# Two pools of the first stretch change places, and the first stretch and batch 1 get a new order

## The chip, the cores and the metric

The kernel runs on one core of a Trainium2 chip. The engines named below are TensorE (PE; its weight loads are listed apart as PEld), VectorE (DVE), ScalarE (ACT), GpSimd (POOL) and SyncE (SP), which here only issues DMAs. The metric is the device time of one execution in microseconds; lower is better. Three executions of the kernel before took 746.87, 747.23 and 748.2 us.

## The reference, cut to what matters

Eight batches of an attention block with a small state, and then a gated feed-forward layer over all 4352 rows that it gives (per batch 512 tokens and 32 state rows, 512 wide):

```python
# x: (B=8, H=8, S=512, D=64), state: (8, 8, 32, 64)
a = softmax(scale * x @ state.T);  xread = a @ state          # tokens read the state
a2 = softmax(scale * state @ x.T); sread = a2 @ x             # the state reads the tokens
rows = concat([xread, sread], axis=2)  -> (B * 544, 512)
xn = rows / rms(rows) * rms_g
g, val = xn @ w_gate, xn @ w_val                              # 512 -> 1536, twice
out = (g * sigmoid(g) * val) @ w_out                          # 1536 -> 512
```

All is float32. The products with w_gate, w_val and w_out are nearly all of the work.

## The kernel before, in words

**Stages.** The kernel works through batch 0 in a first stretch (to about 134 us of the profile), through batches 1 to 7 in seven stretches of about 81 us, and through the state rows of all batches at the end. Since the tokens' reads are `a @ state`, each batch first multiplies the weights with its state (`own_weights`, L753 on PE, copied to a tile `v` by ACT at L765), and then the small matrix `v` with the softmax weights `aT_s`.

**The first stretch** also brings the weights in. They lie in 18 pieces of 1 MB (six pairs of blocks, each gate, val, out). SP loads a piece into one of three `raw` buffers (L241); ACT makes its exponents in two steps (L274 into `lin`, L277 into `ex`), DVE the mantissas (L298) and joins both into the working weight `w_m` or `wo` (L302). A raw buffer is loaded again once its piece is joined, so the load of piece k+3 stands behind the joining of piece k. Each `w_m` is stored back (L305) and fetched again by later batches (L222). For batch 0, `hidden` (L806 on PE, twice a block: gate, then value) fills PSUM banks `pv`, ACT applies silu (L812), DVE multiplies (L816) into `hb`. The projection of batch 0 (L1039 on PE) runs in three groups of blocks; it multiplies blocks of `hb` with blocks of `wo`, and sums of four of them (`group`: POOL at L1023 for the weights, DVE at L1033 for the tokens), and DVE adds the banks up (L1077 to L1088). The last group needs the last two blocks of `hb`.

**What is made for later.** When all weights are joined, DVE makes three sums of `wo` blocks (`weight_sums`, L1114, nine instructions into the tile `wt`), and from `wo` and `wt` the quarter sums for the projections of the later batches (`weight_quarters`, L1226, into three `w2` buffers, which SP stores at L1228 and fetches again at L1217). Batch 1's own token sums (`aT_t`, L828 to L831) are POOL's.

**Batches 1 to 7.** `hidden_seven` runs seven products for each of six pairs of blocks (L910 on PE; ACT copies L957 to L962 and silu L964; DVE additions L973 and L986), `project_twice` the projection as seven outer times seven inner products (L1272 on PE; DVE's quarter sums of tokens L1320 to L1326, half sums L1331; fetches L1217). Beside that DVE, ACT and PE make the next batch's softmax: `x` is turned by DVE (L357), goes out to memory and back in four parts (L359, L364 on ACT's queue, tile `xG`), and PE reads it at L374.

**What sets the order.** Nothing is reordered by a scheduler. Each piece of work is a generator (a stream) named by a letter, and a table of letters says which stream takes its next step: `ORDER` for the first stretch, `FIRST` for batch 1, `PERIOD` for batches 2 to 6. Each engine executes its instructions in that order, and so does SP's queue.

**The places in memory.** Five pools of the first stretch lie one behind the other in the order in which they are opened (L120 to L125): `raws` (three buffers of 8200 bytes per partition), `v_0` (two of 4096: the `v` tiles of batch 0, which L806 reads to its end), `conv` (two of 4096: `ex`), `line` (one of 4096: `lin`), `x_0`. At the first step of a stream `k` (weight sums) or `w` they are closed, and the pools of the later batches are opened on the same place (L1097). The first of these, `late`, holds `wt` (18432 bytes), `hs` (6144) and `aT_t` (3072), 27648 bytes together. Its first instruction waits for the last users of every pool under it.

Of the kernel before, what the change touches and what calls it, by code (L numbers as in the profile page):

```python
# [24 lines left out]
ZERO = 16 * 896  # L25

ORDER = (
    "zzzzaazaaaggggaaaaziizzbzeeeaaaddbbebbaddaabebbsssebzaaaAAAAaAAssabbdAAssdbabbaa"
    "AaAsbbssvbabbebavebbvAddeAehbdhtdeeAAuAdddhAAethuvvveephtddsssWhuesehhssreddstpA"
    "xdvveeWWWuTTrTppxTrrpvpeerrhxppddWAAAAeeddthhAeAAeddStddvvdvhhhuWWxiueppAeeAAddA"  # L30
    "tuhheAddrtuTAeeArxTATTApApeSddSSvxrAvAAvrAppihxShAedppWtheeeuhetdxdvvvddupkkWWWk"
    "kkkkSSShrrSSthhtAAQQQQkpQQxAWuhuTTTSSTAAwrrcppwwwwwxwQQrrSkcpSprrxcQppxwQwcQQ"
)

PERIOD = (
# [4 lines left out]
)  # L40

FIRST = (
    "hhaattavqvhxtaxhahhaauuuqtuqhhtqqtvhqhthhquuqquahuthtqqfuaxhhutxxqqxhthhuaahuhhu"
    "ttthhhqhtxxuukqhkaquuGuvtxhhtaaaukxtaaaGhhtkhhxxhhhGuuuuuttutaaauhhuhuhtuhuutupp"
    "hppppppaaaucuffupkakukkkkppcpppkkpkpppckkaakaalaakkkkkpfkpppcpassaaksaagsppcpkpk"
    "akkkppggappppppppaoogggpsssgcppkakkpssppkooaaassppkskppakkkkoopaafpwwxxxclfwxsxx"
    "coos"
)
LAST = (
    "vhhtnfthhnthxuhguxhtvvhutuhxfhtuthuhhuhhxtuthfxhtuxtxuhxhuhuvtauhhhthxuuthkxthuh"  # L50
# [11 lines left out]
def kernel(  # L62
# [56 lines left out]
    seven["s2"] = ctx.enter_context(tc.tile_pool(name="quarters_h", bufs=2))  # L119
    early = ExitStack()  # L120
    raws = early.enter_context(tc.tile_pool(name="raws", bufs=RAW_AHEAD))
    v_0 = early.enter_context(tc.tile_pool(name="v_0", bufs=2))
    conv = early.enter_context(tc.tile_pool(name="conv", bufs=2))
    line = early.enter_context(tc.tile_pool(name="line", bufs=1))
    x_0 = early.enter_context(tc.tile_pool(name="x_0", bufs=1))  # L125


# [1399 lines left out]
```

## Time and profile before

| | |
|---|---|
| three executions | 746.87, 747.23, 748.2 us; median 747.23 |
| the profiled execution | 747.86 us, of which the span of the core is 746.1 us |
| busy in the span | PE 728.5, DVE 574.4, ACT 350.6, POOL 283.8 us |
| mean granted TensorE clock | 0.993 of full speed |

The span is the time from the first to the last instruction. The profiled execution lies 0.63 us over the median. PE is busy for 98% of the span, so time can be saved only where PE stands still or runs at a lower clock. A row of the timeline has the start and the length in us, engine, line, operation, output and inputs, and in brackets the idle time of that engine just before and what ended it.

### The profile page before, as it was taken

How to read it: one execution, taken by the hardware profiler on the slowest of the kernel's cores; microseconds unless marked ns; L12 is line 12 of the kernel's file. 1: busy time of each engine (PE TensorE's matmuls, PEld its weight loads, DVE VectorE, ACT ScalarE, POOL GpSimd, SP SyncE). 2: the span in 40 equal slices, each digit the busy share in tenths (PEclk: the TensorE clock that was granted, in tenths of full speed). 3: DMA queues.
4: the chain of work that ended last, by engine and by line, in shares of the span. 5: the costliest groups of instructions: out<-in, count | busy, mean ns of one | idle time of the engine just before them, and what ended most of it. 6: DMA issues, size and time to landing. Idle time of an engine off the chain costs nothing.

```text
span 746.1 us, 14468 instructions
## 1 busy us (share of the span) xinstructions
PE 728.5 (98%) x5676; PEld 606.8 (81%) x5676; DVE 574.4 (77%) x972; ACT 350.6 (47%) x610; POOL 283.8 (38%) x376
## 2 busy tenths in 40 slices
PE   8999986999999999999999999999999999999998
PEld 7555554789987898889877997799878987899996
DVE  5878838899946996699848995699569964798862
ACT  5988831256355533654265335552556236511220
POOL 3224023531294126532474228502851267324500
PEclk9999997999999999999999999999999999999999
DMA  7999724785496078706782389318850783063311
GB/s 227 344 317 350 292 114 157 265 308 200 163 283 190 5 304 276 255 11 230 252 309 57 122 312 331 86 36 327 299 185 2 296 265 114 0 223 118 135 51 28
DMA packets 58940, 146.17 MB, mean 196 GB/s; under 512 B 10228, under 2 KB 30200, under 8 KB 51960
## 3 DMA queue, kind: packets, MB, share of 16 engines
q1 hardware_dynamic: 47824, 126.30, 47.5%
q10 hardware_dynamic: 11048, 18.95, 8.5%
q8 instruction: 45, 0.74, 0.4%
q14 instruction: 23, 0.19, 0.1%
HBM read 116.46 MB, written 28.77 MB: 195 GB/s over the span
## 4 chain that ended last, share of the span: by engine, by line
PE 91%; DVE 3%; DMA 3%; ACT 1%; SPq 0%; issue 0%; POOL 0%; DVEq 0%; ACTq 0%
PE f L910 39%; PE f L1272 31%; PE f L1039 5%; PE pv L806 4%; PE pv L753 4%; PE f L1134 2%; PE at L753 2%; DMA raw<-in_moe_w_val_dram 1%; DMA x_b<-in_x_dram 1%; PE at L456 1%; PE at L374 1%; PE f L680 1%; DVE wt L1114 1%; DMA out_dram<-c 1%; DVE w_m L302 1%
## 5 line engine op out<-in xcount | busy, mean ns | idle before, releaser
L910 PE MATMUL f<-aT_s,v 128*128 128x256 f32 x504 | 120.1, 382 | 0.0
L910 PEld LDWEIGHTS f<-aT_s,v 128*128 128x128 f32 x504 | 94.6, 190 | 23.0 <-DVE c L973 5.9
L1300 POOL TENSOR_TENSOR kept<-kept 128x256 f32<-128x256 f32 x28 | 21.2, 756 | 210.7 <-DVE kept L1312 147.1
L973 DVE TENSOR_TENSOR g<-g,f 128x512 f32<-128x512 f32 x84 | 56.7, 685 | 57.6 <-PE f L910 48.6
L910 PE MATMUL f<-aT_t,vs 128*128 128x256 f32 x336 | 86.6, 381 | 0.0
L1272 PE MATMUL f<-w,h 128*128 128x128 f32 x588 | 74.5, 276 | 0.0
L1272 PEld LDWEIGHTS f<-w,h 128*128 128x128 f32 x588 | 69.7, 192 | 4.1 <-DVE eB L662 4.1
L910 PEld LDWEIGHTS f<-aT_t,vs 128*128 128x128 f32 x336 | 63.1, 190 | 10.9 <-issue 1.0
L964 ACT ACTIVATE hb<-g 128x1024 f32<-128x1024 f32 x42 | 44.4, 1058 | 57.3 <-DVE g L973 57.2
L780 POOL TENSOR_TENSOR vs<-v 128x256 f32<-128x256 f32 x42 | 31.3, 746 | 88.5 <-ACT v L765 88.3
L1285 ACT COPY kept<-f 128x512 f32<-128x512 f32 (+1 forms) x56 | 29.3, 532 | 71.3 <-PE f L1272 61.9
L765 ACT COPY v<-pv 128x512 f32<-128x512 f32 x56 | 31.1, 594 | 39.9 <-PE pv L753 39.6
L986 DVE TENSOR_TENSOR hb<-hb,f 128x512 f32<-128x512 f32 (+1 forms) x48 | 31.1, 649 | 18.2 <-PE f L910 18.2
L973 DVE TENSOR_TENSOR c<-c,f 128x512 f32<-128x512 f32 (+1 forms) x48 | 31.3, 653 | 16.4 <-PE f L910 16.2
L910 PE MATMUL f<-aT_s,vs 128*128 128x256 f32 x168 | 43.3, 380 | 0.3 <-ACT c L960 0.3
L910 PE MATMUL f<-aT_t,v 128*128 128x256 f32 x168 | 43.2, 380 | 0.0
L1272 PE MATMUL f<-wo,h 128*128 128x128 f32 x336 | 42.1, 275 | 0.0
L1272 PE MATMUL f<-wo,hb 128*128 128x128 f32 x336 | 42.1, 275 | 0.0
L1272 PEld LDWEIGHTS f<-wo,hb 128*128 128x128 f32 x336 | 40.3, 192 | 0.4
L806 PE MATMUL pv<-aT_s,v 128*128 128x512 f32 x88 | 40.3, 597 | 0.0
L1272 PEld LDWEIGHTS f<-wo,h 128*128 128x128 f32 x336 | 39.8, 192 | 0.0
L986 DVE TENSOR_TENSOR hb<-hb,c 128x512 f32<-128x512 f32 (+1 forms) x48 | 32.9, 685 | 5.7 <-ACT hb L964 4.9
(261 smaller groups left out, 1632.5 us busy)
## 6 DMA issues: line engine op xcount, KB each, us to landing
w_m<-w_d SPq DMA_DIRECT2D x48, 1024.0 KB
w<-t_d SPq DMA_DIRECT2D x49, 576.0 KB
out_dram<-kept SPq DMA_DIRECT2D x30, 256.0 KB
raw<-in_moe_w_val_dram SPq DMA_DIRECT2D x6, 1024.0 KB
raw<-in_moe_w_out_dram SPq DMA_DIRECT2D x6, 1024.0 KB
w_d<-w_m SPq DMA_DIRECT2D x6, 1024.0 KB
x_b<-in_x_dram SPq DMA_DIRECT2D x6, 1024.0 KB
x_d<-xB ACTq DMA_DIRECT2D x6, 1024.0 KB
```

The source lines that it names most:

```text
L753: TE.matmul(out=pv[e][Ns * j:Ns * j + Ns, :], lhsT=stT_g[b][D * e:D * e + D, j, :], rhs=w[D * e:D * e + D, j].rearrange("p m k f -> p (m k ...
L765: SE.copy(v[:, e].rearrange("p m k f -> p (m k f)"), pv[e])
L780: GE.tensor_tensor(out=vs[:, 0], in0=a21, in1=a22, op=ALU.add)
L806: TE.matmul(out=to[0], lhsT=lhs(i, k), rhs=r, start=(i == 0), stop=(i == len(rhs) - 1))
L910: TE.matmul(out=ps[:, i, 0:half], lhsT=l[:, i, :], rhs=r, start=(start and i == 0 and k == 0), stop=(k == len(lhs) - 1), skip_group_check= ...
L964: SE.activation(out=hb[:, 2 * mp:2 * mp + 2, 0:n].rearrange("p m (c t) -> p m c t", c=2), in_=q["g"][:, :, :, 0:half], func=ACTF.Silu if s ...
L973: VE.tensor_tensor(out=to, in0=to, in1=q[ps][:, :, 0:half], op=ALU.add)
L986: VE.tensor_tensor(out=part, in0=part, in1=val, op=ALU.mult)
L1039: TE.matmul(out=bank[:, r, :], lhsT=lhs[:, k, P * r:P * r + P], rhs=rhs[:, k], start=(start and r == 0 and k == 0), stop=(stop and k == 1) ...
L1272: TE.matmul(out=to[half][:, slot, :], lhsT=lhs[:, k, :], rhs=rhs[:, k, :], start=(fresh and n in (0, 4) and k == 0), stop=(k == QM - 1), s ...
L1285: SE.copy(of_half(k, i), banks[name][i])
L1300: GE.tensor_tensor(out=k[:, 4:8:3], in0=k[:, 5:6].to_broadcast([P, 2, QD]), in1=k[:, 4:8:3], op=ALU.add)
```

## The change

Two things. First, the pool `line` is opened ahead of `v_0` and `conv` instead of behind them. The 27648 bytes of `late` then lie over the three `raw` buffers and the first 3 KB of `line`, where they lay over the three `raw` buffers and the first 3 KB of `v_0`. No tile changes its size. Second, the tables `ORDER` and `FIRST` are dealt anew: nearly all streams take the same steps (batch 0 to 1 and the weights' conversion), in another sequence. No instruction is added or removed but for the splitting of runs; `PERIOD`, `LAST` and `STATES` stay.

```diff
 ORDER = (
-    "zzzzaazaaaggggaaaaziizzbzeeeaaaddbbebbaddaabebbsssebzaaaAAAAaAAssabbdAAssdbabbaa"
...
+    "zzzzaazaagaeeaaaazgzzbzaaaebbdeadgbdbbaaedbsssbbzaaaaAAAAAessgdbAbassAAAbbdaaAbb"
...
@@ -119,9 +119,9 @@
     raws = early.enter_context(tc.tile_pool(name="raws", bufs=RAW_AHEAD))
+    line = early.enter_context(tc.tile_pool(name="line", bufs=1))
     v_0 = early.enter_context(tc.tile_pool(name="v_0", bufs=2))
     conv = early.enter_context(tc.tile_pool(name="conv", bufs=2))
-    line = early.enter_context(tc.tile_pool(name="line", bufs=1))
     x_0 = early.enter_context(tc.tile_pool(name="x_0", bufs=1))
```

What the tables do is shown by the order of the instructions on three engines. The names in brackets are the semaphores that an instruction waits for, by the engine that raises them (DMAHW: a DMA).

**DVE, where the weights' last piece is joined (L302 into wo) and the weight sums begin (L1114).** Before:

```order
L302 TENSOR_TENSOR wo<-raw,ex 128x1024 [waits DVE_49,Activation_49]
L816 TENSOR_TENSOR hb<-t,pv 128x512 [waits PE_49,Activation_49]
L1114 TENSOR_TENSOR wt<-wo 128x512 [waits PE_49,DVE_49,Activation_49,Pool_49]
L1114 TENSOR_TENSOR wt<-wo,wt 128x512 [waits DVE_49]
L1114 TENSOR_TENSOR wt<-wo,wt 128x512
L1114 TENSOR_TENSOR wt<-wo 128x512 [waits Pool_49]
```

After:

```order
L302 TENSOR_TENSOR wo<-raw,ex 128x1024 [waits Activation_49]
L1114 TENSOR_TENSOR wt<-wo 128x512 [waits DVE_49]
L1114 TENSOR_TENSOR wt<-wo,wt 128x512 [waits DVE_49]
L1077 TENSOR_TENSOR c_560<-c_560,f 128x512 [waits PE_49]
L816 TENSOR_TENSOR hb<-t,pv 128x512 [waits PE_49,Activation_49]
L1114 TENSOR_TENSOR wt<-wo,wt 128x512
```

The first weight sum no longer waits for PE. Eight of the nine weight sums stood ahead of the last two blocks of hb (L816) before, and seven do now; the L816 of an earlier block is moved in between them.

**PE, the end of batch 0's hidden blocks (L806) and the last group of the projection.** Before:

```order
L806 MATMUL pv<-aT_s,v 128x512 x4
L401 MATMUL at<-part,groups 128x16
L1039 MATMUL f<-wo,hb 128x256 x2
L806 MATMUL pv<-aT_s,v 128x512 x2
L680 MATMUL at<-x_b,e_748 32x64 x32
L325 MATMUL at<-ident,ri 128x128 x4
L1039 MATMUL f<-wo,hb 128x256 x4
L1039 MATMUL f<-group 128x256 x4
```

After:

```order
L806 MATMUL pv<-aT_s,v 128x512 x4
L401 MATMUL at<-part,groups 128x16
L806 MATMUL pv<-aT_s,v 128x512 x2
L1039 MATMUL f<-wo,hb 128x256 x4
L806 MATMUL pv<-aT_s,v 128x512 x2
L1039 MATMUL f<-group,hb 128x256 x4
L1039 MATMUL f<-wo,hb 128x256 x4
L325 MATMUL at<-ident,ri 128x128 x4
```

Behind the last L806 stand now four matmuls on finished sums (L1039 f<-group,hb); before, the L1039 that needs the last two hb blocks came after 36 short ones (L680, L325).

**ACT, batch 1: the last parts of x's way back (L364) and the silu of a pair of blocks (L964).** Before:

```order
L364 DMA xG<-x_d_149 32x4x512
L960 COPY c_1339<-f 128x512
L765 COPY v<-at 128x512 x2
L962 COPY g<-f 128x2x256
L364 DMA xG<-x_d_149 32x4x512 x2
L964 ACTIVATE hb<-g 128x1024
```

After:

```order
L364 DMA xG<-x_d_149 32x4x512 x2
L765 COPY v<-pv 128x512
L962 COPY g<-f 128x2x256
L364 DMA xG<-x_d_149 32x4x512
L964 ACTIVATE hb<-g 128x1024
L364 DMA xG<-x_d_149 32x4x512
```

The last part is issued behind the silu of the third pair of blocks instead of ahead of it. On SP's queue, the load of batch 2's `x` moves ahead of the first store of quarter sums, and in batch 1 the fetch of the fourth set of quarter sums (L1217) stands first, takes one of the three buffers early, and leaves the third fetch to wait until PE is through with the first set; three fetches of 1 MB (L222, for batch 2) stand behind that third fetch now, and stood behind it, without its waiting for PE, before.

More of the change, by code (lines that the diff above doesn't have):

```diff
@@ L27 @@
 ORDER = (
-    "zzzzaazaaaggggaaaaziizzbzeeeaaaddbbebbaddaabebbsssebzaaaAAAAaAAssabbdAAssdbabbaa"
[L29 to L32, printed above, removed]
+    "zzzzaazaagaeeaaaazgzzbzaaaebbdeadgbdbbaaedbsssbbzaaaaAAAAAessgdbAbassAAAbbdaaAbb"
+    "sssbaaevvebbabbbaddbbAvhhAhheeteddeduAAAAdvtpdevveeuhtssepxsAeeddWdhWsuhtAWssAWd"
+    "hrsedvvvurTTppTexTrrrSeppAehAdAddAAxdAAdAeeddAithuppeedWWWWxvhdtvvhiiuAAehthehut"
+    "dhdeuedpSpAAxrAATTTrTArpAAeeddWSdvvvpxeredhhSSAAdptrSpueeSSxShppeedvdhASSdvvhhik"
+    "kAhxtWpupkttkWQkkkQQhSQruuAArrxrQTATTTAWwppxkrwwQQwwwwwppxrrrccppckSSQQQQxcwQ"
 )
@@ L42 @@
 FIRST = (
[L43 to L47, printed above, removed]
+    "haafaaaahqtvvhtthuhuhthhttauqqhhhtxxhhhvluuqqxqquutuuhthqqhxxqthhxaauxtuauthhuah"
+    "htthhhthqqavqqxqqxhghuuuutttxxuhhtkaukkhGGGuaaaaahhhuuxhuutttakuhhhhthaappuuuuuu"
+    "tauhaffauuukkkkppppuppppppppkkakkfcppapkkkpcpakpaacapagkpkkkkkakpppppppssskgakpp"
+    "cppkpgpaaaassaccgoggkkappkpssspkpsppkaaaapsppkkkskopppoafakpkkosoawwxwxxxsxxolcc"
+    "foos"
 )
```

## The prediction

> **What bounds the kernel now.** I read the page first, for which engine is full, then what PE waits for, then the chain of waits around the largest of these waits, and last the stages behind it by windows.
>
> ```profile
> span 746.1 us, 14468 instructions
> PE 728.5 (98%) x5676; PEld 606.8 (81%) x5676; DVE 574.4 (77%) x972; ACT 350.6 (47%) x610; POOL 283.8 (38%) x376
> ```
>
> PE is the bound: 17.6 us of the span are not PE work. The waits of PE, sums and counts:
>
> ```profile
> PE f L1039 <- DVE hb L816: 9.2, 1, 9.2
> PE f L325 <- POOL ri L318: 1.1, 1, 1.1
> PE at L753 <- DVE w_m L302: 0.9, 1, 0.9
> PE f L910 <- ACT c L960: 0.3, 1, 0.3
> ```
>
> One wait is more than half of all. In the chain of waits (start, length, what) it reads:
>
> ```profile
> 106.69 1.73 PE pv L806 x4
> ...
> 108.62 1.47 DVE wt L1114
> ...
> 110.11 1.91 DVE wt L1114 x3
> ...
> 114.22 0.47 DVE w L1226
> ...
> 118.59 0.61 DVE hb L816
> ...
> 119.24 0.80 PE f L1039
> ```
>
> DVE's first weight sum starts when PE's last L806 ends (106.69 + 1.73 = 108.42); DVE then works through its weight and quarter sums, and only behind them comes the product of the last two hb blocks, which PE's L1039 needs. DVE's own timeline shows how long it waited:
>
> ```profile
> 96.66 0.68 DVE L816 TENSOR_TENSOR hb<-t,pv 128x512 f32<-128x512 f32 x1
> 108.62 1.46 DVE L1114 TENSOR_TENSOR wt<-wo 128x512 f32<-128x512 f32 x1 [11.28 <-PE pv L806]
> ```
>
> and the windows what stood beside it, and that PE came back at half its clock (after the length: PE, PEld, DVE, ACT, POOL busy, granted clock, DMA share, GB/s):
>
> ```profile
> 97.30:108.60 11.30, 11.30 (x59) 6.78 (x61) 0.04 (x1) 3.83 (x10) 3.43 (x4) 1.00 0.30 120
> ...
> 119.24:124.40 5.16, 5.16 (x12) 4.17 (x13) 5.09 (x9) 0.00 (x0) 0.36 (x1) 0.50 0.68 198
> 138.60:209.90 71.30, 70.96 (x509) 62.74 (x508) 69.54 (x122) 33.78 (x60) 19.92 (x26) 1.00 0.64 227
> ```
>
> DVE stands still for 11.28 us while PE works, and then PE for 9.2 us while DVE works. The last row matters too: through batch 1 DVE is busy 69.54 of 71.30 us, so there it is nearly as full as PE.
>
> **The change, part by part.**
>
> *The stall.* With `line` under the end of `late`, the first weight sum waits for DVE alone, since `raw` and `lin` are done with when the last piece is joined. So seven weight sums, four quarter sums and two smaller steps move into DVE's 11.28 us. Do they fit? Between the joining and the last two L816, the new order has 7 L1114 at 0.64 (1.91 for three in the chain), 4 L1226 at 0.47 to 0.57, two L816 at 0.61, an L1077 of the same size and two small steps: some 8.8 us. From the joining's end, ahead of the L816 at 96.66, that is 105.5. PE's last L806 ends about where it did, at 108.4: the new order puts L680 and some L1039 ahead of it, and other L1039 behind it, of about the same length together. PE then still has four matmuls `group,hb` (eight in the profile, 1.73 us by the rows below) before it touches the new hb, and L816 takes 0.61. The 9.2 us go whole: −9.2, bounds −9.2 and 0 (the wait as it is). What is late next is DVE's L816 ahead of the last one: ACT has three silu, two table switches and the last exponents in a row there, so the joining may come 1 to 2 us later, and then the last L806 waits for its bank.
>
> *The clock.* After the stall PE runs at 0.50 until 124.4. The same matmuls before and after:
>
> ```profile
> 55.66 1.89 PE L1039 MATMUL f<-wo,hb 128*128 128x256 f32 x8
> 57.39 1.89 PE L1039 MATMUL f<-group,hb 128*128 128x256 f32 x8
> 119.24 3.78 PE L1039 MATMUL f<-wo,hb 128*128 128x256 f32 x8 [9.22 <-DVE hb L816]
> 122.82 2.70 PE L1039 MATMUL f<-group 128*128 128x256 f32 x8
> 125.45 1.09 PE L753 MATMUL pv<-w_m,stT_g 64*32 64x512 f32 x16
> ```
>
> From start to start eight take 57.39 − 55.66 = 1.73; after the stall 122.82 − 119.24 = 3.58 and 125.45 − 122.82 = 2.63. That is 1.85 + 0.90 = 2.75 us, which go with the stall; if a wait of several us stays, they stay: bounds −2.75 and 0. [...]
>
> *The start.* The second half's exponential on ACT now stands ahead of a weight step (L277), and its transposes ahead of L585 on PE:
>
> ```profile
> 17.74 1.16 ACT L277 ACTIVATE ex<-lin,bounds 128x1024 int32<-128x1024 f32 x1
> 18.79 0.62 ACT L546 ACTIVATE eS<-eS 128x512 f32<-128x512 f32 x1
> ```
>
> So the chain that ends in the 1.1 us wait of L325 starts up to 1.05 earlier; DVE's pieces on it are partly put behind others. I take −0.5, bounds −1.1 and +0.5. The 0.9 us at L753 stays: what it waits for hangs, in the chain, on a load of 9.24 us:
>
> ```profile
> 36.88 9.24 DMA raw<-in_moe_w_val_dram
> ```
>
> No load of that stage is moved on SP's queue. The load of batch 2's x, now issued near 100 us, falls where the DMA share is 0.30: nothing. The 0.3 us of L910 on ACT's `c` came from an output transfer that is now issued about 2 us earlier relative to L910: −0.3, bounds −0.3 and 0.
>
> *New waits.* (1) The last L806 behind DVE, above: DVE's steps beside POOL's L1023 are longer:
>
> ```profile
> 108.25 1.28 POOL L1023 TENSOR_TENSOR group<-wo,group 128x512 f32<-128x512 f32 x1
> ```
>
> The one L1114 that ran beside L1023 took 1.46 where three others took 1.91. In the new order two or three L1023 of the last group fall among the weight sums: up to 3 × 0.82 = 2.5 us more for DVE, against a spare of 108.4 − 105.5 = 2.9 us, of which the late joining also takes. I take 0.7, bounds 0 and 2.5. [...] (2) L374 in batch 1. The last part of xG was issued ahead of silu L964, and now behind it:
>
> ```profile
> 153.66 0.96 ACTq L364 DMA_DIRECT2D xG<-x_d  x1
> 155.98 1.06 ACT L964 ACTIVATE hb<-g 128x1024 f32<-128x1024 f32 x1 [2.04 <-DVE g L973]
> 161.84 1.09 PE L374 MATMUL at<-xG,stT 64*32 64x512 f32 x16
> 233.49 1.76 ACTq L364 DMA_DIRECT2D xG<-x_d  x4
> 238.00:239.00 1.00, 1.00 (x7) 0.85 (x6) 0.88 (x2) 0.52 (x2) 0.87 (x2) 1.00 1.06 201
> 239.00:240.00 1.00, 1.00 (x6) 0.90 (x5) 0.48 (x2) 0.53 (x1) 1.00 (x2) 1.00 0.15 25
> ```
>
> Issued at the end of that silu (157.0) it would have 4.8 us until L374. In batch 2 four parts went out by 235.25 and the DMA engines fell quiet at about 239.2, 4 us later; one part behind three needs less, but stores of quarter sums fall beside it. I take 0.3, bounds 0 and 2. (3) The fetch that waits for PE's first set of quarter products:
>
> ```profile
> 178.27 14.09 PE f L1272 x126
> ...
> 180.33 0.32 SPq L1217 DMA_DIRECT2D w<-t_d  x1
> ...
> 182.00:183.00 1.00, 1.00 (x11) 1.00 (x11) 1.00 (x2) 0.16 (x1) 0.00 (x0) 1.00 0.95 373
> 183.00:184.00 1.00, 1.00 (x11) 1.00 (x11) 0.96 (x2) 0.00 (x0) 0.00 (x0) 1.00 0.13 51
> ```
>
> Such a fetch was over some 3 us after its issue; it is needed a whole set of products later (42 matmuls of the profile, a third of 14.09: 4.7 us). Nothing, bounds 0 and 1.5. The three 1 MB fetches behind it are needed only when all seven sets are done, six sets or 28 us later: nothing. (4) DVE in batch 1. It works closely ahead of PE:
>
> ```profile
> 193.45 0.56 DVE L1322 TENSOR_TENSOR h<-h,hs 128x384 f32<-128x384 f32 x1
> 194.11 1.56 PE L1272 MATMUL f<-w,h 128*128 128x128 f32 x12
> ```
>
> L1322 ends 0.1 us before PE needs it. If PE comes 11 us earlier, DVE must too; it does, by the 11.28 us that it no longer waits. Its steps are the same ones in nearly the same sequence. I take 0.2, bounds 0 and 3.
>
> *Sum.* 747.86 (the profiled execution, which is 0.63 over the median) − 9.2 − 2.75 − 0.5 − 0.3 + 0.7 + 0.3 + 0.2 = 736.3 us.
>
> **The rivals.**
>
> (A) *DVE takes the wait back.* Batch 1 leaves DVE 1.8 us in 71, and L374, L1272 and the last L806 each lie within a us or two of their data. If contention with POOL and late xG cost their bounds (2.5 + 2) and the clock stays up, the time is 747.86 − 12.75 + 4.5 = 739.6 and in the worst case, with DVE's 3, 742.6. For it speaks the 69.54 of 71.30; against it that no PE wait of over 0.4 us stands in batch 1 now, with a gap as small.
>
> (B) *The feed falls behind, and it is slower.* DVE now has three L816, paced by six L806 in a row, ahead of the joining of pieces 12 and 13, up to 3 us later than before by my count. Three raw buffers pass a delay on: the load of piece 15 waits for 12, and a load can take 9.24 us. If each of the last L753 waited for its weights, PE would lose a wait and its clock again. The point from which it decides is 12.75 us at the L753s of pieces 13 and 16; with 3.5 us for each of four and as much again for the clock the time is about 749. For it speaks how close the joining of piece 16 came before:
>
> ```profile
> 92.98 1.83 DVE L302 TENSOR_TENSOR w_m<-raw,ex 128x1024 int32<-128x1024 int32 x1
> ...
> 95.70 1.09 PE L753 MATMUL at<-w_m,stT_g 64*32 64x512 f32 x16
> ```
>
> It ended 0.9 us ahead of L753. Against it: of all L753 only one waited for its weights before, and for 0.9 us, and pieces 14 to 17 stand about where they stood among DVE's steps.
>
> (C) *The change does not do what it says:* the sums wait for PE by another way (the store of `v`, a bank), the stall only moves: 747 ± 0.7. Against it: the order shows no semaphore of PE at that instruction.
>
> **How the numbers follow.** Differences under 0.2% (1.5 us) can't be told from no change here. The forecast 0.75, with its own range 734.5 to 738; A 0.16; C 0.04; B 0.05. Faster is forecast and A: 0.91. The range of 8 in 10 reaches down to 734.5 (all new waits zero, the start at its bound) and up to 740.4, which takes in the middle of A.
>
> **What would show it.** Right: no PE wait over 1 us near 110 us; DVE busy between 97 and 108; the granted clock 1.00 from 100 to 130; the first L910 and L1114 each about 11 us earlier. Wrong: a wait of L806 on DVE `hb` or of L753 on `w_m` above 2 us; L374 waiting for a DMA; L1272 waiting for DVE `h` by more than a us; a clock below 1 in any of these.

## The result, and the profile after

The changed kernel took 734.24 us in the median of five executions (733.56 to 735.85), the kernel before beside it 747.22; the ratio is 0.9832, 95% interval 0.9815 to 0.9849, so the change saves 12.6 us (11.3 to 13.8). The ratios compare the means of all executions, not the medians. Two later sets of five gave ratios of 0.9859 (0.9835 to 0.9884) and 0.9842 (0.9824 to 0.9861). The forecast of 736.3 us is a ratio of 0.985. The first median lies 0.3 us under the lower end of the range, those of the later sets (736.01 and 735.15) inside it. The range was built on the profiled execution of before (747.86); the profiled execution of the changed kernel lies inside it.

The profiled execution took 735.58 us, 12.28 less than that of before. From its page, the engines' busy times, and then PE's waits (sum, count, longest):

```profile
span 733.8 us, 14464 instructions
PE 725.0 (99%) x5676; PEld 604.3 (82%) x5676; DVE 571.8 (78%) x972; ACT 350.6 (48%) x610; POOL 289.0 (39%) x376
```

```profile
PE f L325 <- POOL ri L318: 1.1, 1, 1.1
...
PE f L910 <- POOL vs L780: 0.8, 1, 0.8
...
PE at L753 <- DVE w_m L302: 0.3, 1, 0.3
```

The lines left out are waits in the first 24 us. The wait of 9.2 us is gone, and the clock is at 1.00 throughout. Of the two smaller waits that before had, 0.9 at L753 and 0.3 at L910, the one is down to 0.3 (at another L753), and the other is 0.8 us and put down to POOL (wrongly, as the experiments show). The windows of the place of the stall and of batch 1 behind it (length, then PE, PEld, DVE, ACT, POOL busy, granted clock, DMA share, GB/s):

```profile
97.30:127.30 30.00, 29.18 (x213) 19.38 (x201) 26.54 (x44) 5.64 (x14) 15.83 (x17) 1.00 0.62 209
127.30:199.00 71.70, 71.70 (x518) 63.81 (x519) 67.88 (x119) 33.27 (x59) 24.63 (x31) 1.00 0.67 228
```

DVE works where it stood still, and in batch 1 PE is busy in 71.70 of 71.70 us, though DVE is at 67.88. DVE's and PE's rows at the place itself:

```profile
96.95 0.69 DVE L1114 TENSOR_TENSOR wt<-wo 128x512 f32<-128x512 f32 x1
97.67 0.69 DVE L1114 TENSOR_TENSOR wt<-wo,wt 128x512 f32<-128x512 f32 x1
...
98.88 0.68 DVE L816 TENSOR_TENSOR hb<-t,pv 128x512 f32<-128x512 f32 x1
99.48 1.79 DVE L1114 TENSOR_TENSOR wt<-wo,wt 128x512 f32<-128x512 f32 x1
...
106.22 0.68 DVE L816 TENSOR_TENSOR hb<-t,pv 128x512 f32<-128x512 f32 x1
107.09 0.69 DVE L816 TENSOR_TENSOR hb<-t,pv 128x512 f32<-128x512 f32 x1 [0.18 <-PE pv L806]
```

```profile
99.69 1.90 PE L806 MATMUL pv<-aT_s,v 128*128 128x512 f32 x4
...
108.55 1.89 PE L1039 MATMUL f<-wo,hb 128*128 128x256 f32 x8
...
127.29 1.10 PE L910 MATMUL f<-aT_s,vs 128*128 128x256 f32 x4 [0.82 <-POOL vs L780]
```

The first weight sum starts at 96.95, right behind the last joining. The last L816 ends at 107.78, and the L1039 that before stood still for 9.2 us runs at 108.55 without a wait. Not to be overlooked is 99.69: there PE's L806 starts 0.13 us after DVE's L816 has ended (98.88 + 0.68 = 99.56).

**Where the 12.28 us are.** Start of the first L753 into bank `at`: 36.55 before, 36.62 after (+0.07). The wait at the L753 near 50: −0.90. The stall: −9.22. The half clock: PE's busy time behind that first L753 fell from 695.4 to 692.7 us, −2.7 (two of the four kinds of L1039, those that ran behind the stall, from 19.9 to 17.8 and from 12.3 to 11.7). L910: 0.82 for 0.34, +0.48. Together −12.27.

### The profile page after: what moved, and what is told of

Its sections match the earlier page's. It is cut to its first block, busy times and chain, and to the rows that moved or that the text cites. A ratio compares the mean times of both kernels' runs of the same rounds, so it can differ in the third digit from the quotient of the medians.

```text
span 733.8 us, 14464 instructions
## 1 busy us (share of the span) xinstructions
PE 725.0 (99%) x5676; PEld 604.3 (82%) x5676; DVE 571.8 (78%) x972; ACT 350.6 (48%) x610; POOL 289.0 (39%) x376
## 4 chain that ended last, share of the span: by engine, by line
PE 93%; DMA 2%; DVE 1%; POOL 1%; ACT 1%; SPq 0%; issue 0%; ACTq 0%; DVEq 0%; POOLq 0%
PE f L910 40%; PE f L1272 32%; PE pv L806 5%; PE pv L753 3%; PE f L1039 3%; PE f L1134 2%; PE at L753 2%; DMA raw<-in_moe_w_val_dram 1%; DMA x_b<-in_x_dram 1%; PE at L456 1%; PE f L680 1%; PE at L374 1%; PE at L325 0%; ACT ex L277 0%; DVE w L1226 0%
## 5 line engine op out<-in xcount | busy, mean ns | idle before, releaser
L910 PE MATMUL f<-aT_s,v 128*128 128x256 f32 x504 | 120.1, 382 | 0.0
L910 PEld LDWEIGHTS f<-aT_s,v 128*128 128x128 f32 x504 | 94.5, 190 | 23.0 <-issue 5.0
L910 PE MATMUL f<-aT_t,vs 128*128 128x256 f32 x336 | 86.7, 381 | 0.0
L1272 PE MATMUL f<-w,h 128*128 128x128 f32 x588 | 74.6, 276 | 0.0
L1272 PEld LDWEIGHTS f<-w,h 128*128 128x128 f32 x588 | 69.7, 192 | 4.2 <-DVE eB L662 4.1
L910 PEld LDWEIGHTS f<-aT_t,vs 128*128 128x128 f32 x336 | 63.0, 190 | 11.7 <-POOL v L782 2.6
L964 ACT ACTIVATE hb<-g 128x1024 f32<-128x1024 f32 x42 | 44.5, 1058 | 56.4 <-DVE g L973 56.4
L780 POOL TENSOR_TENSOR vs<-v 128x256 f32<-128x256 f32 x42 | 31.4, 748 | 82.3 <-ACT v L765 82.1
L910 PE MATMUL f<-aT_s,vs 128*128 128x256 f32 x168 | 43.2, 379 | 0.8 <-POOL vs L780 0.8
L910 PE MATMUL f<-aT_t,v 128*128 128x256 f32 x168 | 43.1, 379 | 0.0
L1272 PE MATMUL f<-wo,h 128*128 128x128 f32 x336 | 42.1, 275 | 0.0
L1272 PE MATMUL f<-wo,hb 128*128 128x128 f32 x336 | 42.1, 275 | 0.0
L1272 PEld LDWEIGHTS f<-wo,hb 128*128 128x128 f32 x336 | 40.3, 192 | 0.4
L806 PE MATMUL pv<-aT_s,v 128*128 128x512 f32 x88 | 40.5, 599 | 0.0
L1272 PEld LDWEIGHTS f<-wo,h 128*128 128x128 f32 x336 | 39.8, 192 | 0.0
```

What stands on the lines that cost most here:

```text
L780: GE.tensor_tensor(out=vs[:, 0], in0=a21, in1=a22, op=ALU.add)
L806: TE.matmul(out=to[0], lhsT=lhs(i, k), rhs=r, start=(i == 0), stop=(i == len(rhs) - 1))
L910: TE.matmul(out=ps[:, i, 0:half], lhsT=l[:, i, :], rhs=r, start=(start and i == 0 and k == 0), stop=(k == len(lhs) - 1), skip_group_check= ...
L964: SE.activation(out=hb[:, 2 * mp:2 * mp + 2, 0:n].rearrange("p m (c t) -> p m c t", c=2), in_=q["g"][:, :, :, 0:half], func=ACTF.Silu if s ...
L1272: TE.matmul(out=to[half][:, slot, :], lhsT=lhs[:, k, :], rhs=rhs[:, k, :], start=(fresh and n in (0, 4) and k == 0), stop=(k == QM - 1), s ...
```

## The experiments

The first 37 us of an execution vary (PE's waits there for the first loads of `x` sum to 0.2 us in the changed kernel's second set and to 1.8 us with six weight sums twice): the first L753 into `at` started between 35.89 and 38.64 in the profiled executions, whatever the kernel. So beside the median times there stands for each run the part of its span behind that L753, which leaves this out. Each ratio is against executions of the kernel before in the same set.

| kernel | median us | ratio, 95% interval | first L753 | span behind it |
|---|---|---|---|---|
| before | 747.22 | 1 | 36.55 | 709.5 |
| changed | 734.24 | 0.9832 (0.9815 to 0.9849) | 36.62 | 697.2 |
| changed, second set | 736.01 | 0.9859 (0.9835 to 0.9884) | 35.96 | 696.2 |
| changed, third set | 735.15 | 0.9842 (0.9824 to 0.9861) | 37.27 | 697.1 |
| pool order alone | 735.09 | 0.9852 (0.9827 to 0.9877) | 38.64 | 696.6 |
| changed, ORDER of before | 734.89 | 0.9847 (0.9823 to 0.9872) | 36.56 | 696.3 |
| changed, FIRST of before | 736.77 | 0.9859 (0.9835 to 0.9882) | 37.69 | 698.0 |
| before, PE kept busy in the stall | 744.12 | 0.9970 (0.9956 to 0.9984) | 36.79 | 707.0 |
| changed, six weight sums twice | 742.79 | 0.9948 (0.9928 to 0.9968) | 38.29 | 703.6 |
| changed, POOL's sums ahead | 738.17 | 0.9885 (0.9867 to 0.9904) | 36.29 | 699.1 |
| changed, PE kept busy at 27 us | 735.31 | 0.9847 (0.9828 to 0.9866) | 36.17 | 696.1 |
| the same, ORDER of before | 734.55 | 0.9838 (0.9819 to 0.9856) | 35.89 | 696.7 |

### Which part of the change does it: the pools or the tables

Pool order alone, against the kernel before:

```diff
     raws = early.enter_context(tc.tile_pool(name="raws", bufs=RAW_AHEAD))
+    line = early.enter_context(tc.tile_pool(name="line", bufs=1))
     v_0 = early.enter_context(tc.tile_pool(name="v_0", bufs=2))
     conv = early.enter_context(tc.tile_pool(name="conv", bufs=2))
-    line = early.enter_context(tc.tile_pool(name="line", bufs=1))
```

> The new pool order with both tables of before. Theory P (the address overlap alone made the stall): DVE's first L1114 starts when the L816 at 96.66 ends, near 97.3, not at 108.6; the sums that stand ahead of the last two L816 took 9.9 us (108.62 to 118.51), so those two end near 108.5, before PE's L1039 at 110.0. The wait of 9.2 us and the 2.75 us at half clock go, the other waits stay as before (0.9 at L753, 0.3 at L910): 747.2 - 12 = 735.3 us, ratio 0.984, within 0.7 us of the changed kernel. Rival Q (the sums must also be dealt anew, since in the old sequence the last two L816 are late even so): PE waits 1 to 3 us at L1039 and part of the half clock stays: 738 to 741 us.

The other two take the changed kernel and put one table back:

```diff
 ORDER = (
-    "zzzzaazaagaeeaaaazgzzbzaaaebbdeadgbdbbaaedbsssbbzaaaaAAAAAessgdbAbassAAAbbdaaAbb"
...
+    "zzzzaazaaaggggaaaaziizzbzeeeaaaddbbebbaddaabebbsssebzaaaAAAAaAAssabbdAAssdbabbaa"
...
```

> The new pool order and the new FIRST, with the ORDER of before. P: equal to pools_alone within 0.5 us (735.3), since batch 1 shows no wait of PE with either FIRST; the wait of 0.9 us at the L753 near 50 comes back if the order of the first stretch removed it, and is gone if it hung on how fast that load ran by chance. Q: 738 to 741. A rival on batch 1 (the new FIRST needs the earlier start that the new ORDER gives): a wait of 0.5 us or more at L374, L910 or L1272 in batch 1 that the changed kernel does not have.

```diff
 FIRST = (
-    "haafaaaahqtvvhtthuhuhthhttauqqhhhtxxhhhvluuqqxqquutuuhthqqhxxqthhxaauxtuauthhuah"
...
+    "hhaattavqvhxtaxhahhaauuuqtuqhhtqqtvhqhthhquuqquahuthtqqfuaxhhutxxqqxhthhuaahuhhu"
...
```

> The new pool order and the new ORDER, with the FIRST of before. If FIRST is worth nothing, as batch 1 of the changed kernel without PE waits suggests: 734.2 us, as the changed kernel, and the 0.8 us wait of L910 on POOL's vs stays, since it comes out of ORDER. If FIRST carries some of the gain: 735 to 737, with a wait of PE in batch 1 that shows where.

And the changed kernel itself beside them:

> The changed kernel beside the three others on the same chip: 734.2 us, ratio 0.983; both theories expect the same. Its gaps to the other three are what is read.

The pool order alone gives the whole gain: 735.09 us, 0.9852, and 696.6 us behind the first L753, where the changed kernel has 696.2 to 697.2. Its timeline, DVE and then PE, at the old place of the stall:

```profile
98.49 0.68 DVE L816 TENSOR_TENSOR hb<-t,pv 128x512 f32<-128x512 f32 x1
99.09 1.45 DVE L1114 TENSOR_TENSOR wt<-wo 128x512 f32<-128x512 f32 x1
...
109.91 1.28 DVE L816 TENSOR_TENSOR hb<-t,pv 128x512 f32<-128x512 f32 x2
```

```profile
111.71 1.89 PE L1039 MATMUL f<-wo,hb 128*128 128x256 f32 x8
113.44 1.89 PE L1039 MATMUL f<-group 128*128 128x256 f32 x8
```

DVE goes straight from L816 into the weight sums, and the last two L816 end at 111.19, half a us ahead of L1039. Rival Q is out: the sums fit into DVE's old idle time in the old sequence too. With the ORDER of before the time is the same as well. So on top of the new pool order the new tables gain nothing that these runs can show; with the old pool order they were not run. The two tables may belong together: the new ORDER with the old FIRST has PE waits in batch 1 that no other of these four has (0.73 us at L910 for DVE's `c`, 0.36 for ACT's `c`) and 698.0 us behind the first L753, 0.8 to 1.8 more than the changed kernel. That is one profile, and its median is 0.8 us above that of the changed kernel beside it, too little to tell by the times. The wait of 0.9 at the L753 near 50 is there (0.76) with the pool order alone, and gone with the ORDER of before and the new FIRST; since these two differ only in batch 1, the order alone does not decide it; how fast that load ran was not compared. That the ORDER has no part is not shown: two of the five profiles with the ORDER of before have this wait, and none of the seven with the new one.

### Is the half clock a matter of PE's idleness

The kernel before, with 20 products into bank 12 that add nothing (ones by zeros), ahead of the L1039 that waits:

```diff
-...TTTSSTTAAwrrcpp...
+...TTTSSTTAAwZZZZZZZZZZZZZZZZZZZZrrcpp...
...
+    def add_nothing(banks):
+        while True:
+            TE.matmul(out=banks["12"][:, 0, :], lhsT=wake, rhs=bounds[:, 2:3].to_broadcast([P, HD]),
+                      start=False, stop=False, skip_group_check=True)
+            yield
```

> The kernel before, with 20 products of ones by zeros (added into bank 12, whose sum they leave as it is) on PE ahead of the L1039 that waits for DVE; at 0.43 us each they fill some 8.7 of the 9.2 us. Theory K (the half clock comes from PE's idleness): DVE is as late as before, L1039 still starts near 119.3, but at the full clock; the L1039 of the next 5 us take 1.73 us for eight instead of 3.58 and 2.63: 747.2 - 2.75 = 744.5 us, ratio 0.9963. Rival M (the L1039 behind the stall are slow for another reason, their operands or a weight load): 747.2, eight L1039 still in 3.6 us.

```profile
109.77 8.88 PE L1419 MATMUL f<-bounds,wake 128*128 128x256 f32 x40
119.14 1.99 PE L1039 MATMUL f<-wo,hb 128*128 128x256 f32 x8 [0.50 <-DVE hb L816]
121.19 1.99 PE L1039 MATMUL f<-group 128*128 128x256 f32 x8
```

```profile
119.14:124.30 5.16, 5.11 (x40) 3.41 (x48) 5.09 (x9) 0.00 (x0) 0.37 (x1) 1.00 0.66 201
```

DVE is as late as ever, and L1039 still starts at 119.14, but eight of them take 1.99 us instead of 3.78, at a granted clock of 1.00 in the very stretch that had 0.50. The ratio of 0.9970 (0.9956 to 0.9984) is 2.2 us (1.2 to 3.3), and behind the first L753 it is 2.5 us. Theory K holds: of the whole gain some 2.5 us are PE's clock, and most of the rest is the wait.

### How much room DVE has left

The changed kernel, with the first six weight sums done twice:

```diff
-                VE.tensor_tensor(out=dst, in0=a, in1=b, op=op)
+                for again in range(2 if k < 4 else 1): VE.tensor_tensor(out=dst, in0=a, in1=b, op=op)
```

> The changed kernel with the first six weight sums on DVE done twice, all of them ahead of the last two L816: 6 x 0.61 to 0.69 = 3.7 to 4.1 us more on DVE. Theory S (DVE has no spare there; L1039 near 108.5 and, through aT_s and POOL, the first L910 on vs follow it): PE waits near 2.7 us at L1039 and the time rises by 3.6 us, bounds 3.2 and 4.3, to 737.8; if a wait of 2.7 us already drops the clock, by up to 2.6 us more. Rival T (the changed order leaves spare: DVE idles 1.4 and 1.5 us at 116 to 120): 734.2 to 735.2, no wait of over 1 us at L1039.

It took 742.79 us, by the ratios 6.6 to 8.7 us over the changed kernel's three sets (6.4 to 7.4 behind the first L753), about twice what S expected. A row of DVE, PE's rows, and ACT's queue in batch 1:

```profile
103.84 0.68 DVE L816 TENSOR_TENSOR hb<-t,pv 128x512 f32<-128x512 f32 x1
```

```profile
104.57 1.98 PE L806 MATMUL pv<-aT_s,v 128*128 128x512 f32 x4 [3.10 <-DVE hb L816]
...
114.65 1.99 PE L1039 MATMUL f<-wo,hb 128*128 128x256 f32 x8 [0.99 <-DVE hb L816]
```

```profile
147.99 0.82 ACTq L364 DMA_DIRECT2D xG<-x_d  x2
```

```profile
150.03 1.99 PE L910 MATMUL f<-aT_s,v 128*128 128x256 f32 x8 [1.30 <-ACT g L962]
```

S is right that there is no room, but the first victim is another: not L1039, but the L806 at 104.57, which wants the bank that the L816 in the midst of the sums reads. Counted from the first L753 that L816 is 3.29 us later than in the changed kernel, and L806 waits 3.10, so the room there is 0.2 us. L1039 adds 1.0, a `group` sum 0.6. Another 1.3 us are something that nobody had named: `x` of batch 2 goes to memory at 137.93, and the fetch of its first part (L364), which waits for that, is issued only at 147.99; ACT's queue stands at that L364, behind it ACT's copy for L910, and so PE waits. These waits are 6.0 us. PE's busy time behind the first L753 is also 1.2 to 1.4 us longer than in the changed kernel (693.9 us); why is open.

### Can the new 0.8 us be taken away

By the first profile the 0.82 us at L910 come out of POOL's queue, where the second set of `v` sums stands behind the last `kept` sum (L1092), which waits 4.4 us for DVE. One letter is moved:

```diff
-    ...ppxrrrccppckSSQQQQxcwQ
+    ...ppxrrrccppcwkSSQQQQxcQ
```

> The changed kernel with one letter of ORDER moved: POOL's second set of v sums (L780 to L783) stands ahead of its last kept sum (L1092), which waits for DVE. Theory V (PE's 0.8 us at L910 near 127 is only this place in POOL's queue): POOL does the sums in its idle 4.4 us from 120.7, the wait goes and nothing follows: 733.4 us, 0.8 under the changed kernel. Rival W (the wait moves on, to the product behind it or to DVE's work beside POOL): 734.2, with a new wait of PE in the next 10 us.

It was not faster but, as it seems, slower: 738.17 us, 0.9885 (with an interval that overlaps that of the changed kernel's second set), and 1.9 to 2.9 us more behind the first L753. POOL does the sums in its idle time, from 120.3 to 124.2, and the same L910 waits all the same, 0.95 us. SP, ACT and PE in this run:

```profile
121.05 0.55 SPq L1382 DMA_DIRECT2D out_dram<-c  x1
```

```profile
126.36 0.59 ACT L960 COPY c<-f 128x512 f32<-128x512 f32 x1 [3.23 <-DMA out_dram<-c]
```

```profile
127.09 1.10 PE L910 MATMUL f<-aT_s,vs 128*128 128x256 f32 x4 [0.95 <-ACT c L960]
```

The L910 adds into the bank that ACT's L960 copies out, and L960 writes the buffer `c` whose output store was issued at 121.05 and is read until about 126.3. That chain stands in the changed kernel too, and in its second profile it can be told apart from POOL. SP, ACT, PE and POOL there:

```profile
120.71 0.55 SPq L1382 DMA_DIRECT2D out_dram<-c  x1
```

```profile
124.60 0.58 ACT L960 COPY c<-f 128x512 f32<-128x512 f32 x1 [1.80 <-DMA out_dram<-c]
```

```profile
125.65 1.03 PE L910 MATMUL f<-aT_s,vs 128*128 128x256 f32 x4
```

```profile
125.76 0.72 POOL L780 TENSOR_TENSOR vs<-v 128x256 f32<-128x256 f32 x1
```

L910 starts before the L780 that it was said to wait for. POOL and ACT in the first profile:

```profile
126.43 0.72 POOL L780 TENSOR_TENSOR vs<-v 128x256 f32<-128x256 f32 x1
```

```profile
126.56 0.59 ACT L960 COPY c<-f 128x512 f32<-128x512 f32 x1 [3.10 <-PE f L910]
```

So POOL never was the cause: L780 (126.43 + 0.72) and L960 (126.56 + 0.59) happened to end at the same 127.15, and the releaser that the profile infers was the wrong one of two. The same holds one step back: L960 is put down to PE's L910 there, which it can't need, since it starts ahead of the same L910 (124.68) in the second profile. The trace's semaphores have the last landing of the store at 126.46 in the first profile, 124.50 in the second and 126.26 in this run, each 0.1 us before L960. Theory V falls with its premise. What sets this wait is how long the store takes, 3.9 us (120.71 to 124.60) with no wait in the second profile, 5.2 (121.38 to 126.56) with 0.82 us in the first, 5.3 here with 0.95. The other 1.64 us of this run are those of the run before it, again: the return of `x` (L364, issued at 142.01, in the changed kernel at 139.21) holds up ACT's queue.

```profile
143.99 1.99 PE L910 MATMUL f<-aT_s,v 128*128 128x256 f32 x8 [1.64 <-ACT g L962]
```

Rival W expected no gain and a new wait within 10 us, and it came 17 us later. Why it is 10 us from the store of `x` to the issue of its first fetch in these two kernels, and 7.3 (131.95 to 139.21) to 8.5 in the three profiles of the changed one, stays open.

### The 1.1 us at the start

In three of the ten profiled executions in which PE waits 1.08 us at the L325 near 27, PE's clock fell behind it. Two products of ones fill the wait:

```diff
+        if h:
+            ps = fy.tile([P, 2, P], F32, name="f")
+            for i in range(2):
+                TE.matmul(out=ps, lhsT=wake, rhs=wake.unsqueeze(1).to_broadcast([P, 2, P]), start=True, stop=True)
         rp = along_rows(ri, HT, fz, "f")
```

> The changed kernel with two products of ones (0.43 us each, into a bank that nothing else uses then) on PE ahead of the second L325, where PE waits 1.08 us for POOL's ri near 27. Seen so far: in three of nine profiled executions PE ran at clock 0.50 for some 4 us behind that wait (eight L374 in 1.96 us, not 1.09), in six it did not. Theory H (this wait, in a stretch where PE has little else, lets the clock fall in some executions and not in others): the wait shrinks to 0.2 us, no execution falls, the upper half of the changed kernel's times (735.6 to 737.0) goes: median near 734.2, highest under 736, against a median near 735.7 and a highest of 737 for the changed kernel beside it. Rival L (the upper half comes from how fast the first loads run): medians equal, both spread over 3 us.

The same in the kernel with the ORDER of before:

> The same two products in the kernel with the new pool order, the new FIRST and the ORDER of before, which had the lowest median beside the changed kernel (734.9 against 736.0) and no wait of PE behind 28 us. H: median near 734.0, highest under 736, so this would be the fastest of all; its part behind the first L753 on bank at stays at 696.3 us. L: 734.9 with single executions at 737.

The control:

> The changed kernel beside the two others on the same chip: median 734.2 to 736.0 as before, single executions up to 737; its gap to start_kept is what is read. H: start_kept 1 to 1.5 us lower in the median; L: no gap.

```profile
26.33 1.03 PE L606 MATMUL f<-wake 128*128 128x256 f32 x4
27.58 0.43 PE L325 MATMUL f<-ident,ri 128*128 128x128 f32 x2 [0.22 <-POOL ri L318]
27.94 1.09 PE L374 MATMUL at<-xT,stT 64*32 64x512 f32 x16
```

The wait shrinks to 0.22, and none of the eight executions with these products took over 735.95 us. But the profiled execution of the changed kernel beside them shows no fall either, and its median (735.15) is no higher. The gain that H expected can't be measured here, since no execution of the changed kernel beside them fell: their mean clocks are 0.999 and 1.000. In the set with the pool order alone many did. Of its 20 executions of four kernels, nine had a mean clock of 0.998 or less (3.4 us at half clock are 0.0023 of the span), and took 735.84 to 737.7 us, 737.0 in the mean; the other eleven took 733.94 to 736.01, 734.9 in the mean. So a fall goes with some 2 us, as H has it, and part of the gaps between the medians of that set is how many executions fell (three of five of the changed kernel and of the one with the FIRST of before, two and one of the others). That the products keep the clock up at this place is not shown. The lowest median of all beside the changed kernel, 734.55 with the ORDER of before, is not distinguishable from it (0.9838, 0.9819 to 0.9856, against 0.9842), so no version is shown to beat the changed kernel.

## Why the prediction was right, and where it was not

**The stall (−9.2): right, size and reason.** Without `v_0` under `late` the weight sums wait for nothing but DVE. The prediction credited the new ORDER with fitting the work into DVE's idle time; the pool order alone does it.

**The clock (−2.75): right.** 2.7 by PE's busy time behind the first L753, 2.5 in the run with PE kept busy.

**The start (−0.5): wrong, it is 0.** The first L753 into `at` starts at 36.62 instead of 36.55. The chain that I shortened isn't the one that ends there: the L325 at its end does start 0.22 us earlier (27.74), but that L753 now waits 0.26 us for a joining, and the chain behind it begins with a load at 23.60 that takes 9.07 us. In the profiles this L753 starts anywhere between 35.89 and 38.64.

**The 0.9 us at L753 "stays": wrong.** It is gone in the changed kernel's first profile, there again (0.76) with the pool order alone, and 0.57 at another L753 in the third set. So it comes and goes between executions; what part the order has is not shown.

**The 0.3 us of ACT's `c` (−0.3): right in mechanism, wrong in sign.** The wait is for the output store, as the prediction had it, but it is 0.82 in the first profile, 0.30 in the third set and nothing in the second. The step that failed is the 2 us by which the store was to be issued earlier: before it was issued at 133.97, 0.48 us ahead of the first L910 (134.45), and now at 121.38, 0.15 ahead of it (121.53).

**New waits (+0.7, +0.3, +0.2 = 1.2): too high, and at the wrong places.** The last L806 (105.10) did not wait for DVE; the one that comes closest is an earlier one, at 99.69, with at most 0.13 us to spare. One L1114 did take longer beside POOL's L1023 (1.79 for 0.69), which is 1.1 of the 2.5 us of the bound, and DVE's spare took it up. L374 never waited for xG; where xG was late, in two of the experiments, it was ACT's queue that stood, and an L910 that waited. L1272 did not wait for a fetch, nor for DVE.

So the sum was 11.55 and the profile gave 12.28: the start missed by 0.57 and the store by 0.78 the one way, the 0.9 and the new waits' 1.2 the other. That these errors of 1.35 and 2.1 us nearly cancel is luck; that the two large terms came out is not.

**The rivals.** C fell with the first profile. B did not occur: no L753 waited over 0.8 us for its weights in any run with the new pool order. A, that DVE takes the wait back, did not occur but is close: six more sums on DVE cost the kernel some 7 us. The prediction's price for it, a us of PE for a us of DVE, was too low for these sums: DVE was busy for 5.3 to 6.4 us more behind the first L753, not for about 4 (beside POOL's L1023 two of them took 3.31 us, where two take 1.29), and the time at which `x` comes back holds up ACT's queue. B's price was summed wrongly: 3.5 us for each of four L753 and as much again for the clock would be 763 us; its 749 holds 14 us once.

## What to carry to other kernels

Where an engine stands still at the first use of a tile, look at what lay at that address before: here the first instruction of a pool opened over several old ones waited for the last user of all it covers (DVE for 11.28 us), and changing the order of two pools gave the whole gain, and reordering the work on top of it gave nothing more that could be measured. A gain from a wait of several us on PE can be the wait and then the clock behind it (here 9.2 and some 2.5 us), and a few products that add nothing show which is which. And before a step is moved for a wait of under 1 us, take a second execution of the same kernel: a releaser that is named there in one profile only need not be the cause.

## What the runs showed of the hardware

**How long PE ran at half the clock.** Before, windows of 2 us around the stall (PE idle from 110.0 to 119.24):

```profile
114.00:116.00 2.00, 0.00 (x0) 0.00 (x0) 1.90 (x6) 0.00 (x0) 0.00 (x0) 0.55 0.00 0
...
122.00:124.00 2.00, 2.00 (x6) 1.64 (x5) 2.00 (x5) 0.00 (x0) 0.00 (x0) 0.50 0.55 189
124.00:126.00 2.00, 2.00 (x22) 1.20 (x29) 1.00 (x2) 0.00 (x0) 1.80 (x3) 0.89 0.08 28
```

A mean of 0.55 in 2 us is 1.8 us at 0.50, and 0.89 is 0.44 us; with the 8 us between them PE was at half clock for 10.2 us, from 114.2 to 124.4 (the trace's own record of the clock gives 10.24 us). In the first 5.0 of them it stood still and in the last 5.2 it worked; only these cost time, 2.7 us by its busy time. In the kernel with the FIRST of before, behind the wait of 1.08 us at 27:

```profile
26.00:28.00 2.00, 0.92 (x8) 0.41 (x6) 1.86 (x5) 2.00 (x5) 1.16 (x1) 0.93 0.94 336
28.00:30.00 2.00, 2.00 (x18) 0.34 (x17) 1.36 (x2) 1.97 (x3) 1.15 (x1) 0.50 1.15 407
30.00:32.00 2.00, 2.00 (x7) 1.72 (x8) 1.85 (x3) 1.69 (x2) 0.12 (x1) 0.72 0.91 284
```

By the same count that is 0.28 + 2.0 + 1.12 = 3.4 us, and 3.4 us too with the pool order alone (0.70, 0.50, 0.94) and with the six sums (0.59, 0.56). With the FIRST of before and with the pool order alone L374 takes 1.96 us there, and 1.09 in the kernel before and in the changed one (28.32, 28.10). Why the clock was down for 3.4 us in these three executions and for 10.2 behind the stall is not shown.

**Behind which waits the clock fell.** Behind the wait of 9.2 us PE ran at 0.50. Behind one of 3.1 us it ran at 1.00, in the profiled execution of the run with six more sums:

```profile
102.00:104.00 2.00, 0.00 (x0) 0.00 (x0) 2.00 (x3) 0.10 (x1) 0.77 (x1) 1.00 0.96 351
104.00:106.00 2.00, 1.43 (x4) 0.72 (x5) 1.97 (x4) 0.00 (x0) 0.00 (x0) 1.00 1.07 346
```

But two of the six executions of that kernel, which were not profiled, had a mean clock of 0.993, as low as the kernel before; no execution of the changed kernel was under 0.997. And in three profiled executions of ten the clock fell behind a wait of only 1.08 us, in a stretch of small products and transposes.

So the length of one wait does not tell in these runs whether the clock falls: 1.08 us went with a fall in three profiled executions and without one in seven, 3.1 us without one in the only profile that has it. From 26 to 28 us PE was busy for 0.92 us both with the FIRST of before, where the clock fell (0.93, then 0.50), and in the changed kernel's first profile, where it stayed at 1.00. What decides it is not shown.

**DVE's and POOL's sums took longer beside each other.** In the changed kernel POOL's L1023 of 97.71 took 1.78 us, where the one of 98.11 in the kernel before, while DVE stood still, took 1.28; beside it ran the L1114 that ended at 98.36 (97.67 + 0.69). And the L1114 of 99.48 took 1.79, 1.11 more than the one of 101.19 (0.68, with POOL idle), beside the next L1023 (99.45 to 100.72, 1.27). So each time one of the two took longer, by 0.5 or 1.1 us, and the other did not; what decides which, the traces do not show.
